# A delta-rule and router kernel whose first stage is put in order by a list scheduler instead of hand-interleaved generators

## The chip, the core and the metric

The kernel runs on one core of a Trainium2 chip. A core has five instruction streams that run side by side and wait for one another through semaphores: TensorE (PE in the profile; PEld is its weight loading), VectorE (DVE), ScalarE (ACT), GpSimd (POOL) and SyncE (SP, which here only issues transfers). SBUF is the on-chip memory of 128 partitions, PSUM the accumulators of TensorE in eight banks. The metric is the device time of the whole program in microseconds (us).

## What is computed

The reference first runs a delta rule over 768 tokens for each of 4 batches and 8 heads of width 48, then sends each token's 384 numbers (8 heads x 48) to its two best of 8 experts.

```python
# delta rule: q, k, v (4, 8, 768, 48), beta (4, 8, 768)
k_n = k / (norm(k) + 1e-6)
for t in range(768):
    y[t] = q[t] @ state
    state = state + beta[t] * outer(k_n[t], v[t] - k_n[t] @ state)
# router: x is y as (3072, 384)
noisy = x @ w_gate + log1p(exp(x @ w_noise)) * noise
top2 and their softmax weights of each token
out[token] += weight * (relu(x @ w1[e]) @ w2[e])      # for its two experts e
```

## The kernel before, in words

The program has two stages. **Stage 1** is the delta rule together with the router's choice; **stage 2** is the eight experts, whose source the change does not touch.

Stage 1 cuts the tokens into 12 chunks of 64. A *unit* is one chunk of one pair of batches (two units a chunk, 24 in all), and a *step* is four units, that is two chunks (six steps, s = 0 to 5). All that depends on k and q alone can be done ahead; only the state must go from chunk to chunk. The pieces are:

- `turned(k)` and `products`: TensorE transposes k (tile `p_t`), ScalarE copies it out (`kT`), TensorE multiplies it with itself (`p_k`), ScalarE copies a part to `at` and the 32-wide diagonal blocks to `gd`.
- `invert(s)`: once a step, VectorE inverts 1024 triangular 32x32 blocks, one column after the other. It transposes `gd` into `t`, finds the lengths of the k (through ScalarE) and the factors `d`, has GpSimd make `low_d`, multiplies `t` by it, and then runs 30 columns of two instructions (`part<-t`, `t<-t,part`). The result is scaled (`scaled`) and transposed twice, into `tt` and `tb`.
- `join(n)`: for each unit, ScalarE copies `tt` into the 64x64 inverse (`w64`, called `w` in the rows), TensorE multiplies `at` by `tb` (`p_x`, first round), ScalarE takes it out negated (`x`), TensorE multiplies again (`p_x`, second round) and ScalarE puts it into `w`.
- `within(n)`: q is transposed (`qT`), multiplied with k (`p_q`), masked by VectorE (`qk`).
- `scale` and `recur`: GpSimd scales `v`; TensorE computes what the state already knows (`p_b`), VectorE subtracts it from `v`, TensorE solves with `w` (`p_u`), ScalarE copies out `u`, TensorE forms the state's increment (`p_s`), VectorE adds it to the state `st`, and GpSimd spreads `st` into the block-diagonal `wide`. This is the chain from chunk to chunk.
- `answer(n)`: TensorE forms the result (`p_y`, from `wide` and from `u`), ScalarE copies `y`, TensorE transposes it (`p_xt`) and multiplies by the gate weights (`p_l`, in the same tile), ScalarE copies the logits.
- `route(s)`: some 25 small VectorE instructions pick the two experts, TensorE counts earlier tokens of each expert (`p_at`), and GpSimd writes the rows into `rows_x` with eight indirect DMAs (`spread`).

Stage 2 reads `rows_x` back (`xr`), so it starts only after the last `spread` has landed.

In what order an engine gets these pieces is set in two places. The source writes them by generators: the loop over chunks calls `take(inverse, 9)`, `take(answers, 3)` and the like between the parts of `recur`, and so mixes inverse, answers, joins and routes by hand. The framework then reorders each engine's instructions by its own estimates. PSUM is shared by two pools: two tiles of one bank (`psum1`) and three of two banks (`psum2`), each given out in the order of the source. At the start ScalarE's queue issues the 16 loads of `beta_b`, and SP issues everything else: k, q and v, the zero-filling of `rows_x` (eight DMAs), the first expert's weights and the zero-filling of the output.

## Time and profile before

| | us |
|---|---|
| runs | 1102.34, 1102.88, 1099.51 |
| median | 1102.34 |
| the profiled execution, its own time | 1099.18 |
| its span | 1097.5 |
| stage 1, until the last count `p_at` starts | 491.9 |
| from there to the end of the span | 605.6 |
| TensorE busy in the span | 889.9 (81%) |
| VectorE busy | 320.2 (29%) |
| ScalarE busy | 253.9 (23%) |
| GpSimd busy | 238.5 (22%) |

The shares are averages over two unlike stages: TensorE is busy nearly all of stage 2, and in stage 1 the work is spread over four engines that hand it on. So the stages are to be read apart. The clock that a row calls PEclk is the one granted to TensorE, as a share of its full speed.

### The profile page before, as it was taken

To read this page: it belongs to the slowest core of one execution; us is meant where nothing else is said; L and a number is where in the kernel's file an instruction comes from. 1 tells how busy PE (TensorE), PEld (TensorE's weight loads), DVE (VectorE), ACT (ScalarE), POOL (GpSimd) and SP (SyncE) were. 2 spreads that over 40 slices of the span, in tenths; PEclk is the share of its full clock that TensorE was granted. 3 is DMA by queue.
4 is the path that set the end of the run, shared out by engine and by line. 5 is a ranking of instruction groups with operands and counts; after the bars stand their busy time and mean duration, and the time that the engine had idled before them with its cause. 6 is when DMAs were issued, how large, how long until landed. Compare 5 with 4: busy or idle time off the path is not lost. (4 is left out here: it accounts for less than half of the span.)

```text
span 1097.5 us, 20220 instructions
## 1 busy us (share of the span) xinstructions
PE 889.9 (81%) x8670; PEld 609.6 (56%) x8670; DVE 320.2 (29%) x916; ACT 253.9 (23%) x621; POOL 238.5 (22%) x297
## 2 busy tenths in 40 slices
PE   3348147786977869672999999999999999999994
PEld 2347046675866758662555555555555555555552
DVE  1777753274573761312002011020120201202000
ACT  3354234442535415110201102002011020110200
POOL 4201111413214231306013012121130121302211
PEclk9657558675576855755999999999999999999997
DMA  5896202312212110106424114241141312301100
GB/s 105 245 365 194 43 2 46 101 36 72 44 31 84 37 63 13 60 1 215 139 86 158 60 45 147 79 143 48 73 155 72 120 56 86 117 8 39 44 23 26
DMA packets 119763, 95.54 MB, mean 87 GB/s; under 512 B 84558, under 2 KB 109676, under 8 KB 119664
## 3 DMA queue, kind: packets, MB, share of 16 engines
q1 hardware_dynamic: 108784, 65.63, 20.5%
q0 software_dynamic: 9984, 28.42, 7.6%
q8 instruction: 70, 1.15, 0.4%
q14 instruction: 29, 0.24, 0.1%
q10 hardware_dynamic: 896, 0.10, 0.1%
HBM read 60.10 MB, written 35.60 MB: 87 GB/s over the span
## 5 line engine op out<-in xcount | busy, mean ns | idle before, releaser
L747 PE MATMUL p_h<-xe,w1e 128*128 128x416 f32 x768 | 270.3, 513 | 6.3 <-DVE xe L741 6.3
L772 PE MATMUL p_o<-w2e,hT 128*128 128x384 f32 x768 | 249.0, 486 | 0.0
L747 PEld LDWEIGHTS p_h<-xe,w1e 128*128 128x128 f32 x768 | 145.3, 190 | 127.0 <-issue 119.7
L772 PEld LDWEIGHTS p_o<-w2e,hT 128*128 128x128 f32 x768 | 145.9, 190 | 102.2 <-issue 2.5
L751 ACT ACTIVATE hT<-p_h 128x416 f32<-128x416 f32 x128 | 66.2, 517 | 491.5 <-PE p_h L747 475.9
L776 DVE SCALAR_TENSOR_TENSOR sums<-p_o,gate,sums 128x384 f32<-128x384 f32 x48 | 29.7, 618 | 449.8 <-PE p_o L772 449.8
L807 POOL DMA_INDIRECT out_dram<-sums,index x56 | 55.1, 984 | 405.0 <-DVE sums L776 382.5
L180 POOL DMA_INDIRECT rows_x<-y,slot x48 | 49.7, 1035 | 91.7 <-issue 42.0
L798 POOL DMA_INDIRECT sums<-out_dram,index x56 | 55.9, 999 | 56.0 <-issue 40.0
L352 DVE TENSOR_TENSOR t<-t,part 128x30 f32<-128x30 f32 (+9 forms) x180 | 61.2, 340 | 4.8
L348 DVE TENSOR_TENSOR part<-t 128x30 f32<-128x30 f32 (+9 forms) x180 | 60.9, 339 | 4.8
L285 PE MATMUL p_q<-qT,kT 64*64 64x64 f32 x768 | 19.0, 258 | 51.1 <-ACT qT L277 49.7
L377 ACT COPY w<-tt 32x256 f32<-32x256 f32 x96 | 38.6, 402 | 55.7 <-DVE tt L363 54.4
L430 PE MATMUL p_y<-u,qk 64*64 64x48 f32 x768 | 45.9, 296 | 1.7 <-issue 1.7
L489 PE MATMUL p_u<-v,w 64*64 64x48 f32 x768 | 39.7, 269 | 9.0 <-ACT y L437 7.1
L285 PEld LDWEIGHTS p_q<-qT,kT 64*64 64x64 f32 x768 | 16.5, 166 | 54.6 <-ACT qT L277 53.0
L430 PEld LDWEIGHTS p_y<-u,qk 64*64 64x64 f32 x768 | 41.9, 212 | 7.1 <-issue 7.1
L463 POOL TENSOR_TENSOR v<-v,norms 128x384 f32<-128x384 f32 x24 | 21.1, 891 | 105.4 <-DMA v<-in_v_dram 90.1
L489 PEld LDWEIGHTS p_u<-v,w 64*64 64x64 f32 x768 | 37.2, 186 | 11.7 <-ACT y L437 6.6
L519 POOL COPY wide<-st 64x384 f32<-64x384 f32 x44 | 23.0, 522 | 91.4 <-DVE st L516 75.6
L383 PE MATMUL p_x<-tb,at 32*32 32x32 f32 x768 | 22.9, 226 | 23.3 <-DVE tb L364 21.5
L737 PE MATMUL p_xt<-ident,xr 128*128 128x128 f32 (+1 forms) x168 | 21.8, 285 | 19.4 <-DMA xr<-rows_x 19.4
(134 smaller groups left out, 862.4 us busy)
## 6 DMA issues: line engine op xcount, KB each, us to landing
w1e<-in_moe_w_dram SPq DMA_DIRECT2D x8, 1536.0 KB
w2e<-in_moe_w_dram SPq DMA_DIRECT2D x8, 1536.0 KB
rows_x<-empty SPq DMA_DIRECT2D x8, 1358.0 KB
xr<-rows_x SPq DMA_DIRECT2D x8, 1164.0 KB
kp<-in_k_dram SPq DMA_DIRECT2D x48, 96.0 KB
qp<-in_q_dram SPq DMA_DIRECT2D x48, 96.0 KB
v<-in_v_dram SPq DMA_DIRECT2D x48, 96.0 KB
out_dram<-empty SPq DMA_DIRECT2D x1, 4608.0 KB
```

The source lines that it names most:

```text
L180: d = nc.gpsimd.indirect_dma_start(out=rows_x, out_offset=bass.IndirectOffsetOnAxis(ap=slot, axis=0), in_=rows, in_offset=None,).ins
L285: nc.tensor.matmul(out[rows_of[b], z, j], lhsT[rows_of[z], j, rows_of[b]], rhs(rows_of[z], j, b), start=(j == 0), stop=(j == NP - 1), skip ...
L348: nc.vector.tensor_tensor(out=part, in0=t[:, j + 1 :, j, None].to_broadcast(shape), in1=t[:, None, j, 0:j].to_broadcast(shape), op=ALU.mult,)
L352: nc.vector.tensor_tensor(out=t[:, j + 1 :, 0:j], in0=t[:, j + 1 :, 0:j], in1=part, op=ALU.add)
L377: nc.scalar.copy(w64[rows, :, cols], tt[rows])
L430: nc.tensor.matmul(p_y[b, h], qk[b, h % 2, h // 2], u[b, h], start=(c == 0 and h == 0), stop=(h == H - 1), skip_group_check=True,)
L489: nc.tensor.matmul(p_u[b, h], w64[b, h], r[b, h], start=(h == 0), stop=(h == H - 1), skip_group_check=True,)
L747: nc.tensor.matmul(p_h, w1e[:, do, fo * 128 : (fo + 1) * 128], xe[:, do, cols], start=(do == 0), stop=(do == KT - 1),)
L751: nc.scalar.activation(hT[:, fo, cols], p_h, ACTF.Relu)
L772: nc.tensor.matmul(p_o, hT[:, fo, i * 128 : (i + 1) * 128], w2e[:, fo], start=(fo == 0), stop=(fo == FT - 1),)
L798: nc.gpsimd.indirect_dma_start(out=got, out_offset=None, in_=out, in_offset=bass.IndirectOffsetOnAxis(ap=index, axis=0), bounds_check=N - ...
L807: nc.gpsimd.indirect_dma_start(out=out, out_offset=bass.IndirectOffsetOnAxis(ap=index, axis=0), in_=got, in_offset=None, bounds_check=N - ...
```

## The change

The change writes stage 1 as some 1340 *jobs*. A job names an engine, a cost in us, what it reads and writes, the PSUM bank it opens, uses or closes, and sometimes a due time; its `emit` holds the instructions. `Jobs.order` is a list scheduler: it keeps a clock for each engine, takes again and again the job that could start first (among those within 0.05 us, the one due earliest), and gives it a free PSUM bank out of four pairs (tiles `pair_112` to `pair_115` in the rows below). The jobs are then emitted in the order of their planned starts, and `tc.manual_schedule` keeps that order on TensorE, ScalarE, VectorE and SP. GpSimd is not in that list, so there the framework goes on choosing.

Besides that:

- the 16 loads of `beta_b` go from ScalarE's queue to SP's, and half of step 0's k loads (four DMAs) go to ScalarE's;
- the zeroing of the borders of `qp` and `w64` goes from GpSimd to VectorE;
- in step 0 half of the `gd` copies and the `low_d` multiply are VectorE's;
- `tb` is transposed ahead of `tt`;
- logits and slots have two buffers each.

```diff
-        psum1 = ictx.enter_context(
-            tc.tile_pool(name="psum1", bufs=2, space=bass.MemoryType.PSUM)
+        psum = ictx.enter_context(
+            tc.tile_pool(name="psum_d", bufs=1, space=bass.MemoryType.PSUM)
         )
-        psum2 = ictx.enter_context(
-            tc.tile_pool(name="psum2", bufs=3, space=bass.MemoryType.PSUM)
-        )
+        jobs = Jobs([psum.tile([128, 2, 512], FP32, name=f"pair{i}") for i in range(4)])
...
-            nc.scalar.dma_start(out=beta_b[i * H : (i + 1) * H], in_=by_block[b, n, c, u])
+                jobs.add(
+                    SP, 0.7,
+                    lambda i=i, at=(b, n, c, u): nc.sync.dma_start(
+                        out=beta_b[i * H : (i + 1) * H], in_=by_block[at]
+                    ),
+                    writes=[("beta", i)], lands=2.5,
+                )
...
+                engine = ACT if name == "k" and n < US and i else SP
+                queue = nc.scalar if engine == ACT else nc.sync
...
+                on, copy = (DVE, nc.vector.tensor_copy) if s == 0 and x % 2 else (
+                    ACT, nc.scalar.copy
+                )
...
+            on = (DVE, 1.25, v_) if s == 0 else (POOL, 2.4, nc.gpsimd)
...
-            nc.vector.transpose(out=tt.rearrange("p h i -> p i h"), in_=scaled)
-            nc.vector.transpose(
-                out=tb.rearrange("p h j -> p j h"), in_=scaled.rearrange("p i j -> p j i")
+            jobs.add(
+                DVE, 1.95,
+                lambda: v_.transpose(out=tbs.rearrange("p h j -> p j h"),
+                                     in_=scaled.rearrange("p i j -> p j i")),
+                reads=["low_d"], writes=["tb"],
+            )
+            jobs.add(
+                DVE, 1.95,
+                lambda: v_.transpose(out=tts.rearrange("p h i -> p i h"), in_=scaled),
+                reads=["low_d"], writes=["tt"],
...
+                        POOL, 1.3, lambda i=i, to=to: spread(ys(s)[:, i], to[:, i : i + 1]),
+                        reads=[("slot", s % 2), meta, ("num", s % 2), ("y", s % 2, i), "clear"],
...
-                if i == 0:
-                    take(answers, 3)
-                    if grams:
-                        products(grams[0])
-                    take(inverse, 9)
-                    take(joins, 2)
-                    take(routes, 3)
...
+            for n in units:
+                join(n)
+            for n in units:
+                recur(n)
+                answer(n)
+            route(s)
+        with tc.manual_schedule(
+            engines={
+                mybir.EngineType.PE, mybir.EngineType.Activation, mybir.EngineType.DVE,
+                mybir.EngineType.SP,
+            }
+        ):
+            jobs.run()
```

The scheduler's inner loop, cut to its core:

```python
for engine in self.ENGINES:
    at = []
    for i in could[engine]:
        start = max(free[engine], ready[i])
        if jobs[i].opens:
            start = max(start, room[0])          # when a PSUM bank comes free
        at.append((start, jobs[i].due, i))
    if at:
        soon = min(at)[0] + self.PATIENCE
        pick = min((x for x in at if x[0] <= soon), key=lambda x: x[1:])
        best = min(best or (1e9,), pick)
```

Three places show how the order moves. In each row stand the line, the operation, and the tile written and the tiles read. First ScalarE's queue at the program's start, before:

```order
L941 UNCONDITIONAL_BRANCH
L247 DMA beta_b<-in_beta_dram 8x6x32 x16
L640 ACT_TABLE_LOAD
L277 COPY kT<-p_t 128x512 x2
L305 COPY at<-p_k 128x256
```

And ScalarE's queue at the start now:

```order
L1227 UNCONDITIONAL_BRANCH
L954 ACT_TABLE_LOAD
L416 DMA kp_116<-in_k_dram 64x8x48
L416 DMA kp_117<-in_k_dram 64x8x48
L416 DMA kp_118<-in_k_dram 64x8x48
L416 DMA kp_119<-in_k_dram 64x8x48
L438 COPY kT_182<-pair_112 128x512
L438 COPY kT_183<-pair_112 128x512
```

Four transfers stand where sixteen stood, and the load of the activation table comes first.

Second, TensorE from a step's first `p_x` (line 383 before, 594 now) on, in step 3. Before, up to the first results `p_y`:

```order
L383 MATMUL p_x<-tb,at 32x32 x32
L285 MATMUL p_b<-st_3378,kT 64x48 x7
L392 MATMUL p_x<-w_0_147,x 32x32 x16
L392 MATMUL p_x<-w_1_150,x 32x32 x16
L285 MATMUL p_b<-st_3378,kT 64x48 x2
L383 MATMUL p_x<-tb,at 32x32 x16
L285 MATMUL p_b<-st_3378,kT 64x48 x5
L383 MATMUL p_x<-tb,at 32x32 x16
L285 MATMUL p_b<-st_3378,kT 64x48 x2
L285 MATMUL p_b<-st_3399,kT 64x48 x2
L392 MATMUL p_x<-w_2_153,x 32x32 x16
L285 MATMUL p_b<-st_3399,kT 64x48 x14
```

Now, from the same place to the first `p_s` (line 707; `p_b` is line 449 with `st`, `p_u` is line 689):

```order
L594 MATMUL pair_112<-tb,at_194 32x32 x16
L594 MATMUL pair_114<-tb,at_195 32x32 x16
L449 MATMUL pair_113<-st_0_220,kT_185 64x48 x16
L594 MATMUL pair_114<-tb,at_196 32x32 x16
L606 MATMUL pair_112<-w_0_148,x_215 32x32 x16
L606 MATMUL pair_114<-w_1_149,x_216 32x32 x16
L594 MATMUL pair_112<-tb,at_197 32x32 x16
L689 MATMUL pair_115<-v_178,w_0_148 64x48 x16
L689 MATMUL pair_115<-v_179,w_1_149 64x48 x16
L707 MATMUL pair_113<-u_212,kp_116 64x48 x16
```

The groups of 16 stay whole, and `p_u` follows the joins of its own two units, where before the answers of the chunk ahead (`p_y`, `p_xt`) came between.

Third, GpSimd between an inverse's `low_d` (line 336 before, 531 now) and its neighbours; `L180` and `L319` are the indirect DMAs of `spread`. Before, around the `low_d` of the fifth inverse and up to its end, where GpSimd sets the diagonal of `t`:

```order
L519 COPY wide_0_171<-st_3399 64x8x48 x2
L336 TENSOR_TENSOR low_d<-low,d 128x1024
L463 TENSOR_TENSOR v<-v,norms 128x384
L519 COPY wide_1_168<-st_3960 64x8x48 x2
L463 TENSOR_TENSOR v<-v,norms 128x384
L519 COPY wide_1_174<-st_3981 64x8x48 x2
L180 DMA rows_x<-y,slot_4093 24576x388
L180 DMA rows_x<-y,slot_4099 24576x388
L356 MEMSET t 128x32
```

Now, from the end of the third inverse to the start of the fourth:

```order
L558 MEMSET t 128x32
L732 COPY wide_0_166<-st_1_218 64x8x48 x2
L660 TENSOR_TENSOR v_180<-v_180,norms_236 128x384
L660 TENSOR_TENSOR v_181<-v_181,norms_236 128x384
L732 COPY wide_0_172<-st_1_221 64x8x48 x2
L319 DMA rows_x<-y_224,slot_0_262 24576x388
...
L319 DMA rows_x<-y_224,slot_1_263 24576x388
L531 TENSOR_TENSOR low_d<-low,d 128x1024
L732 COPY wide_1_167<-st_2_219 64x8x48 x2
```

Before, the `spread` of a step came behind a `low_d`; now all eight stand ahead of one here. Ahead of the third inverse's `low_d` four of eight stand, ahead of the fifth's six, ahead of the sixth's three. On VectorE the multiply that needs `low_d` has the rest of its inverse and the second chunk of the step behind it:

```order
L525 STREAM_TRANSPOSE norms_237<-norm 128x32
L719 TENSOR_TENSOR st_2_219<-pair_115,st_1_218 128x384
L538 TENSOR_TENSOR t<-t,low_d 128x1024
L719 TENSOR_TENSOR st_2_222<-pair_112,st_1_221 128x384
L679 TENSOR_TENSOR v_180<-v_180,pair_115 128x2x4x48
```

The multiply is the third row; the state of the second pair of batches (`st_2_222`) and the next chunk's `v` wait behind it.

## Rows read from the trace of the kernel before

**Rows 1.** The span in 40 equal slices, busy share in tenths, from the page
```profile
PE   3348147786977869672999999999999999999994
DVE  1777753274573761312002011020120201202000
PEclk9657558675576855755999999999999999999997
```

**Rows 2.** Busy time by stretch: engine busy us (instructions), granted clock, DMA share, GB/s
```profile
core 0: us, PE busy (x) PEld busy (x) DVE busy (x) ACT busy (x) POOL busy (x), PEclk, DMA share, GB/s
187.00:252.80 65.80, 52.02 (x1166) 45.91 (x1166) 33.48 (x111) 24.60 (x66) 17.95 (x22) 0.68 0.26 62
252.80:324.90 72.10, 57.78 (x1166) 51.63 (x1166) 39.93 (x123) 30.90 (x82) 19.06 (x23) 0.59 0.21 52
451.30:492.00 40.70, 28.73 (x303) 25.09 (x303) 5.59 (x35) 6.36 (x18) 7.76 (x8) 0.54 0.11 40
520.00:1097.50 577.50, 555.69 (x1809) 314.34 (x1807) 65.51 (x155) 66.18 (x128) 107.45 (x109) 0.99 0.25 83
```

**Rows 3.** The same view, two stretches in which TensorE hardly waits
```profile
286.00:304.00 18.00, 17.67 (x381) 15.73 (x377) 12.15 (x37) 6.92 (x19) 2.35 (x1) 0.50 0.05 11
306.00:318.00 12.00, 9.73 (x313) 8.46 (x312) 6.39 (x21) 8.17 (x22) 2.64 (x4) 0.98 0.26 51
```

**Rows 4.** Timeline, start: start us, us, engine, line, operation, tiles, [idle before <-releaser]
```profile
0.81 12.32 ACTq L247 DMA_DIRECT2D beta_b<-in_beta_dram  x16
13.17 1.28 ACT L640 ACT_TABLE_LOAD   x1 [13.17 <-DMA beta_b<-in_beta_dram]
25.21 1.91 DVE L315 STREAM_TRANSPOSE t<-gd 128x1024 f32<-128x1024 f32 x1 [22.28 <-ACT gd L308]
33.54 1.83 DVE L342 TENSOR_TENSOR t<-t,low_d 128x1024 f32<-128x1024 f32 x1 [3.08 <-POOL low_d L336]
38.90 21.70 SPq L174 DMA_DIRECT2D rows_x<-empty  x8
62.00 1.91 DVE L364 STREAM_TRANSPOSE tb<-scaled 128x1024 f32<-128x1024 f32 x1
109.61 1.89 DVE L364 STREAM_TRANSPOSE tb<-scaled 128x1024 f32<-128x1024 f32 x1
403.77 1.97 DVE L364 STREAM_TRANSPOSE tb<-scaled 128x1024 f32<-128x1024 f32 x1
```

**Rows 5.** Timeline, ScalarE and TensorE around 150 us, where TensorE waits longest
```profile
149.97 0.82 ACT L377 COPY w<-tt 32x256 f32<-32x256 f32 x2 [32.46 <-DVE tt L363]
151.45 1.13 PE L285 MATMUL p_q<-qT,kT 64*64 64x64 f32 x32 [30.71 <-ACT qT L277]
```

**Rows 6.** Groups by line in 0 to 500 us: busy us, mean ns | idle before
```profile
L352 DVE TENSOR_TENSOR t<-t,part 128x30 f32<-128x30 f32 (+9 forms) x180 | 61.2, 340 | 4.8
L377 ACT COPY w<-tt 32x256 f32<-32x256 f32 x96 | 38.6, 402 | 55.7 <-DVE tt L363 54.4
L409 DVE TENSOR_TENSOR qk<-p_q,mask 128x512 f32<-128x512 f32 x24 | 16.4, 682 | 6.3 <-PE p_q L285 6.2
L336 POOL TENSOR_TENSOR low_d<-low,d 128x1024 f32<-128x1024 f32 x6 | 14.1, 2346 | 28.0 <-DVE d L334 28.0
L516 DVE TENSOR_TENSOR st<-p_s,st 128x384 f32<-128x384 f32 x20 | 10.9, 543 | 77.5 <-PE p_s L507 77.5
```

**Rows 7.** Timeline, the end of stage 1 and the start of stage 2
```profile
476.83 0.90 PE L442 MATMUL p_xt<-ident,y 128*128 128x128 f32 x3 [0.58 <-ACT y L437]
483.26 0.90 PE L442 MATMUL p_xt<-ident,y 128*128 128x128 f32 x3 [0.58 <-ACT y L437]
491.90 0.60 PE L593 MATMUL p_at<-r_taken,mask_u 128*128 128x32 f32 x2 [5.65 <-DVE y L535]
495.84 0.96 POOL L180 DMA_INDIRECT rows_x<-y,slot  x1 [30.68 <-issue]
497.11 0.96 POOL L180 DMA_INDIRECT rows_x<-y,slot  x1 [0.30 <-issue]
```

More of the change, by code (lines that the diff above doesn't have):

```diff
@@ new lines, in ring, with per_head, two_banks @@
+        def ring(shape, name, n, zero=None, engine=nc.gpsimd):
+            made = [sb(shape, f"{name}{i}") for i in range(n)]
+            for t in made:
+                for part in zero(t) if zero else ():
+                    engine.memset(part, 0.0)
+            return lambda i: made[i % n]
+        def per_head(p):
+            return p.tile[:, 0 : H * D].rearrange("p (h d) -> p h d", d=D)
+        def two_banks(p, cols):
+            return p.tile[:, :, 0 : NP * cols].rearrange("p z (j d) -> p z j d", d=cols)
@@ new lines, in second, with joined @@
+            def second():
+                for h in range(H):
+                    for up, dn in pairs:
+                        nc.tensor.matmul(
+                            p_x()[up, 1, h], x[dn, h], w64[dn, h, Q:C],
+                            start=(h == 0), stop=(h == H - 1), skip_group_check=True,
+                        )
+            def joined():
+                for up, dn in pairs:
+                    nc.scalar.copy(w64[up, :, Q:C], p_x()[up, 1])
+            w, below = ("w", n % NW), [("w", n % NW, lo) for lo in (Q, C + Q)]
@@ new lines, in multiply @@
+            def multiply():
+                p_l = p_xt.tile[:, KT * 128 : KT * 128 + 2 * E]
+                for do in range(KT):
+                    nc.tensor.matmul(
+                        p_l, xTs(n)[:, do], router["wgn"][:, do],
+                        start=(do == 0), stop=(do == KT - 1),
+                    )
+            reads = [("qT", n % NQ), ("qk", n % NQ), ("u", n % N_U)]
+            if c:
+                reads.append(("wide", z, c % 2))
+            jobs.add(PE, 2.2 if c else 1.3, of_chunk, reads=reads, opens=p_y)
@@ new lines, in answer @@
+            jobs.add(
+                ACT, 0.5,
+                lambda: nc.scalar.copy(y_n, per_head(p_y).rearrange("p h d -> p (h d)")),
+                writes=[y_key], closes=p_y,
+            )
+            jobs.add(PE, 0.6, turn, reads=[y_key], opens=p_xt)
+            jobs.add(
+                ACT, 0.5,
+                lambda: nc.scalar.copy(
+                    xTs(n), p_xt.tile[:, 0 : KT * 128].rearrange("p (t i) -> p t i", i=128)
+                ),
+                writes=[xT_key], uses=p_xt,
+            )
@@ new lines, in answer @@
+            jobs.add(PE, 1.0, multiply, reads=[xT_key, "wgn"], uses=p_xt)
+            jobs.add(
+                ACT, 0.2,
+                lambda: nc.scalar.copy(
+                    logits(s)[:, i],
+                    p_xt.tile[:, KT * 128 : KT * 128 + 2 * E].rearrange(
+                        "p (x e) -> p x e", e=E
+                    ),
+                ),
+                writes=[("logits", s % 2, i)], closes=p_xt,
+            )
+        small = {x: sb([128, Q], x) for x in ("ss", "root", "norm", "d")}
@@ new lines, in rows, with weights @@
+            def rows():
+                p_at = p.tile[:, 0 : US * E].rearrange("p (u e) -> p u e", e=E)
+                vv(at, p_at, part[:, None, :].to_broadcast([128, US, E]), ALU.add)
+                for hit, to in zip((hit0, hit1), slot):
+                    vv(mine, hit, at, ALU.mult)
+                    nc.vector.tensor_reduce(out=row, in_=mine, axis=AX.X, op=ALU.add)
+                    nc.vector.tensor_copy(to, row)
+            def weights():
+                nc.vector.tensor_scalar(
+                    out=den, in0=p1, scalar1=1.0, scalar2=1e-9, op0=ALU.add, op1=ALU.add
+                )
+                nc.vector.reciprocal(den, den)
+                vv(gate1, p1, den, ALU.mult)
+                vv(gate0, den, gate1, ALU.subtract)
@@ new lines, in counted @@
+            def counted():
+                nc.vector.tensor_reduce(
+                    out=r_count, in_=taken.rearrange("p u e -> p e u"), axis=AX.X, op=ALU.add
+                )
+                vv(before, before, r_count, ALU.add)
+            every_logit = [("logits", s % 2, i) for i in range(US)]
+            meta = ("meta", s % 2)
+            jobs.add(
+                POOL, 0.2,
+                lambda: nc.gpsimd.tensor_copy(
+                    num, number.rearrange("p c u -> p (c u)")[:, every]
+                ),
+                writes=[("num", s % 2)],
+            )
```

871 lines of the change are left out of this document (490 added, 381 removed).

## The prediction

> **What bounds the kernel now.** I read the 40 slices first, since the shares of the whole span mix two stages. TensorE is at 9 tenths or more from the 19th slice on and at a clock of 9 tenths, and between 3 and 8 before that, at 4 to 7 tenths [rows 1]. So the second stage is bound by TensorE (555.69 of 577.50 us busy at a clock of 0.99 [rows 2]), the change leaves its source alone, and I carry its time over. The first stage ends when the last count `p_at` starts, at 491.90, and the last `spread` and the read-back of `rows_x` follow from there [rows 7]. Whatever is gained must bring that moment forward.
>
> Inside stage 1 the landmark is the end of `tb`, which is the end of an inverse: 63.9 for the first, 111.5 for the second and 405.7 for the sixth [rows 4]. Four steps lie between the last two, 73.6 us each. No engine needs that long. TensorE is busy 52.02 of 65.80 us and 57.78 of 72.10, VectorE 33.48 and 39.93, ScalarE and GpSimd less [rows 2]. The rest is handing on in a poor order. The plainest case: ScalarE stood 32.46 us before a `w` copy whose `tt` was not there, with the copy of `qT` queued behind it, and TensorE waited 30.71 us for that `qT` [rows 5]. A better order can win only up to what the slowest engine needs alone, so I work out that bound for each engine, and then the path in the order that the change fixes.
>
> **TensorE's price depends on its clock.** The two middle stretches of [rows 2] hold the same 1166 matmuls: 52.02 us at 0.68 and 57.78 at 0.59. A line in one over the clock through both (14.2 + 25.7/clock) gives 39.9 us a step wholly at 2.4 GHz and 65.6 at 1.2. What the clock will be is the largest unknown. In 286 to 304 TensorE was busy 17.67 of 18 us and had 0.50, that is the lower level throughout; in 306 to 318, busy 9.73 of 12, it had 0.98 [rows 3]. So a full queue did not bring the high level there, and I take about 0.62, the middle of the two steps: 55.6 us.
>
> The Trainium skill ("TensorE: Matmul & The Clock Gate", "Loop structure matters more than you think") says that whether matmuls stay at the fast clock is a matter of keeping them back to back. By that rule the denser order would lift the clock; the first row of [rows 3] disagrees, and the rule's result is the first rival.
>
> **The start.** ScalarE issues 16 `beta_b` loads in 12.32 us, loads its table at 13.17 and only then copies; `t<-gd` starts at 25.21 after 22.28 us of idle VectorE [rows 4]. Now ScalarE issues four loads (3.1 us at 0.77 each) and the table (1.28), so it is free at about 5.5. When k lands the rows do not show, only that it was there by 14.46, when the first copy followed right behind the table; with half of its loads on each queue I take 6 to 10. The copies took it some 11 us (14.46, right behind the table, to 25.21); with half of the `gd` copies on VectorE 7 to 9. That puts `t<-gd` between 13 and 19 (23 if k really needs till 14.46); I take 16, a gain of 9. The betas on SP (16 more issues, about 12 us) are needed only in the lengths, behind `t<-gd`. The zeroing that VectorE takes over lies in its idle 22 us; were that cover gone it would cost about 2.
>
> From `t<-gd` to the end of `tb` the first inverse took 38.7 us. The wait of 3.08 for GpSimd's `low_d` [rows 4] goes, a multiply on VectorE of about 1.5 comes, and `tt` (1.9) moves behind `tb`: 35.2, so `tb` ends at 51. The second inverse took 47.6 us after the first; I keep that and add 2 for the loads of `v`. SP now has those 16 betas and step 1's q ahead of the 21.70 us of `rows_x` clears [rows 4], and step 1's `v` behind the clears and the weights; that could cost 0 to 10, once. The second `tb` ends at 101.
>
> **A step in the new order.** VectorE works in the fixed order, so I add it up from one `tb` to the next. Behind the multiply `t<-t,low_d` lie: multiply, the 30 columns (60 instructions of 0.34 us [rows 6] and the gaps between them) and `scaled`, together 25.9 (from 33.54 to 62.00 is 28.5, less one `qk` of 0.68 and `tt` of 1.9); `tb` 1.9; one `st`, two `v` (0.54 each; the subtraction is of the same shape) and four `qk` (0.68 each), 4.3; and the router's small operations, 4.8 of the 5.59 that the last stretch shows [rows 2, 4, 6]. That is 36.9 us.
>
> Ahead of that multiply stand `tt`, `t<-gd`, one `st`, two `v` and the gates: 6.6 us. Only then can GpSimd start the `spread`s, because the gates are part of the rows, and GpSimd's order, which the change leaves to the framework, puts 4, 8, 6 and 3 of them ahead of the next `low_d`. One `spread` takes 1.27 us from start to start [rows 7], `low_d` 2.35 [rows 6]. So the multiply starts at 9.0 + 1.27n after `tb`, and a step takes at least 51.0, 56.1, 53.5 and 49.7 us. Without any `spread` ahead it would be some 46: this is a **new wait** that the change makes, and behind it on VectorE stand the second `st` and the second chunk's `v`, hence TensorE's second `p_u`.
>
> TensorE needs 55.6 at the middle clock, and cannot have zero idle time: at each `tb` it waits for the first `x` and `w` copies, and ScalarE's 16 `w` copies of 0.40 a step [rows 6] stand between join and `p_u`. I put 2 to 3 us on that. **TensorE is later than VectorE's sum in each step**, so the steps are 58, 59 (where eight `spread`s also hold VectorE), 58, and 54 for the last, in which no k of a further step is multiplied. That is 229 in place of 294, and the sixth `tb` ends at 330 in place of 405.7.
>
> **The end of stage 1.** From there before needed 86.2 us to `p_at`, since work of the chunk before was still queued ahead. Now the last step's joins, two chunks of `p_b`, `p_u` and one `p_s` (18 to 24 us by clock, estimated from TensorE's steps), four answers, and the router are left. An answer took 6.43 us from `p_xt` to `p_xt`, with 0.58 waiting for `y` [rows 7]; with two of them in flight I count 5 each. The router waited 5.65 before `p_at` [rows 7]. 21 + 20 + 1.5 + 6 is about 49, so `p_at` starts at 379.
>
> **The sum.** 491.9 less 379 is 113. The profiled execution took 1099.18 us (span 1097.5), so the same execution would take 986. The median of the three runs, 1102.34, lies 3.2 above the profiled one; I say 988.
>
> **The rivals.**
>
> *The clock rises.* If fewer gaps keep TensorE at 2.4 GHz, its 39.9 us a step vanish behind VectorE, whose four steps give 210 by the floors above, 216 with 1.5 us of waiting each. The end shrinks to 40, since the matmuls of the last answers are halved. `p_at` then starts at 101 + 216 + 40 = 357: **967**. For it: 0.98 in 306 to 318. Against it: 0.50 in the densest stretch, and 0.54 in the last [rows 2, 3]. Two in ten.
>
> *TensorE stays at 1.2 GHz.* 65.6 a step and 1 of handing on, 62 in the last, 55 at the end: 101 + 262 + 55 = 418, a gain of 74: **1028**. For it: the same 0.50 row. The order groups `p_x`, `p_u` and `p_y`, which is what ran there. Two in ten.
>
> *Slower than before.* The place is GpSimd's queue between two inverses. The order is fixed on four engines and cannot give way there: `low_d` waits for all `spread`s ahead of it, these for the router's gates, the router for the last answer's logits, and VectorE's multiply holds the second chunk. If that ring closes, TensorE stands still while VectorE waits and the other way about. It decides once the four steps reach 491.9 - 49 - 101 = 342, 85.5 each: TensorE at 65.6 and idle 20 us in every step, as long as GpSimd takes for eight `spread`s, `low_d` and what is ahead (19). At 88 a step the result is **1110**. Against it: only one of four steps has all eight ahead, and TensorE has products of the next steps queued meanwhile. Five in a hundred.
>
> *The late loads of `v`.* All of the 10 us instead of 2 gives 996; this is inside the forecast. That the order isn't what the change says is excluded for the four fixed engines by the order of the built program; what is not fixed, GpSimd's, is priced above.
>
> **How the numbers follow.** Forecast 0.53, high clock 0.2, low clock 0.2, slower 0.05, and 0.02 for a result within 0.3% of before (3.3 us, about what a measurement of this kernel can tell from no change), the point at which the ring almost closes. Range: the high clock's 967 less 15, for a start 5 us earlier and one `spread` fewer ahead in each step; the low clock's 1028 plus 8 for the late `v`: 952 to 1036. Faster 0.93, within 0.02, slower 0.05.
>
> **What would show it.** Right: `t<-gd` at 13 to 19 and the first `tb` at about 51; steps of 54 to 60 between `tb`s; TensorE busy over 90% of a step at a clock near 0.6; VectorE's longest idle in front of `t<-t,low_d`, released by GpSimd, longest in the fourth inverse; stage 2 unchanged at about 606 us from `p_at`. Wrong: a clock of 0.9 in stage 1 with VectorE full (first rival), steps of 66 at 0.5 (second), VectorE and TensorE idle by turns over 15 us a step (third), or `t<-gd` still after 20.

## The result, and the profile after

| | before | changed |
|---|---|---|
| runs, us | 1102.34, 1102.88, 1099.51, 1097.93 | 1009.23, 1008.37, 1008.77, 1004.28 |
| median | 1100.92 | 1008.57 |
| the profiled execution (its span) | 1099.18 (1097.5) | 1009.23 (1007.5) |
| `p_at` of the last step starts | 491.9 | 404.1 |
| from there to the end of the span | 605.6 | 603.4 |

The changed kernel takes 0.9155 of the time [0.912, 0.919]: 92 us less, where 114 (to 988) had been forecast. Of the 90 us between the two spans 87.8 are the earlier end of stage 1.

The busy shares of the 40 slices of the changed kernel, in tenths (a slice is now 25.2 us):

```profile
PE   4368778676968767199999999999999999999995
DVE  6957768496785832210200200201201102002001
PEclk7757667596875858599999999999999999999998
```

Against [rows 1], VectorE stands at 4 to 9 in the first 14 slices (stage 1 ends in the 17th), and TensorE at much the same tenths as before, for fewer slices. The stretches between the ends of `tb`, and stage 2, in the columns of [rows 2]:

```profile
core 0: us, PE busy (x) PEld busy (x) DVE busy (x) ACT busy (x) POOL busy (x), PEclk, DMA share, GB/s
0.00:50.70 50.70, 21.22 (x432) 17.15 (x432) 39.39 (x123) 19.64 (x47) 13.18 (x39) 0.73 0.56 102
50.70:109.90 59.20, 45.10 (x938) 41.62 (x938) 39.09 (x111) 29.14 (x79) 5.62 (x7) 0.63 0.99 333
109.90:173.20 63.30, 50.62 (x1194) 46.14 (x1193) 44.87 (x123) 30.34 (x81) 24.04 (x29) 0.68 0.33 76
173.20:235.00 61.80, 45.89 (x1170) 41.45 (x1169) 43.91 (x123) 30.93 (x82) 19.59 (x23) 0.75 0.28 67
235.00:295.00 60.00, 45.86 (x1167) 41.07 (x1166) 43.56 (x123) 30.89 (x82) 19.24 (x23) 0.75 0.23 57
295.00:355.50 60.50, 46.18 (x1066) 40.62 (x1064) 45.35 (x122) 23.89 (x62) 19.84 (x23) 0.70 0.22 55
355.50:404.10 48.60, 34.34 (x868) 31.21 (x868) 12.62 (x39) 18.90 (x52) 10.77 (x14) 0.68 0.10 35
430.00:1007.50 577.50, 558.70 (x1817) 316.07 (x1815) 67.00 (x158) 66.18 (x128) 108.97 (x110) 0.99 0.26 84
```

A step went from 73.6 us to some 61. No engine fills one: TensorE is busy 45.9 of 61.8 at a clock of 0.75, VectorE 43.9. What VectorE waits for is seen in its timeline around the second of the four steps' multiplies by `low_d`, with the first `t<-gd`, the last multiply and the last `p_at` (idle time before and its releaser in brackets):

```profile
16.73 1.91 DVE L495 STREAM_TRANSPOSE t<-gd 128x1024 f32<-128x1024 f32 x1
...
194.46 0.56 DVE L719 TENSOR_TENSOR st<-pair,st 128x384 f32<-128x384 f32 x1 [10.06 <-PE pair L707]
194.93 1.22 DVE L538 TENSOR_TENSOR t<-t,low_d 128x1024 f32<-128x1024 f32 x1
...
307.55 1.18 DVE L538 TENSOR_TENSOR t<-t,low_d 128x1024 f32<-128x1024 f32 x1
...
404.13 0.64 PE L882 MATMUL pair<-r_taken,mask_u 128*128 128x32 f32 x2 [5.62 <-DVE r_taken L833]
```

`t<-gd` answers to 25.21 in [rows 4], `p_at` to 491.90 in [rows 7]. The multiply at 194.93 comes 21.7 us after its `tb`, but it has no wait of its own: VectorE stood 10.06 us before the state `st` ahead of it, for the products of TensorE. So the longest wait was where the prediction put it, and the engine that came last was another.

What TensorE did in those 10 us stands in its timeline, here with GpSimd's (the lines 689 and 707 are `p_u` and `p_s`):

```profile
181.66 1.75 PE L689 MATMUL pair<-v,w 64*64 64x48 f32 x26
183.69 0.43 PE L689 MATMUL pair<-v,w 64*64 64x48 f32 x3 [0.28 <-issue]
...
185.86 0.36 PE L689 MATMUL pair<-v,w 64*64 64x48 f32 x3 [0.96 <-issue]
187.29 0.46 PE L689 MATMUL pair<-v,w 64*64 64x48 f32 x4 [1.06 <-issue]
...
191.60 1.09 PE L689 MATMUL pair<-v,w 64*64 64x48 f32 x15 [0.47 <-issue]
193.26 1.10 PE L707 MATMUL pair<-u,kp 64*64 64x48 f32 x32 [0.57 <-ACT u L696]
...
180.15 1.03 POOL L319 DMA_INDIRECT rows_x<-y,slot  x1 [3.60 <-DVE before L833]
...
189.15 0.97 POOL L319 DMA_INDIRECT rows_x<-y,slot  x1 [0.30 <-issue]
190.19 2.34 POOL L531 TENSOR_TENSOR low_d<-low,d 128x1024 f32<-128x1024 f32 x1
```

The 64 matmuls of one `p_u` came in pieces of 3 to 5 with about 1 us between them, for which the trace shows no releaser, and took 11 us, while GpSimd issued eight `spread`s (180.15 to 190.1). The same happens, with pauses of 0.3 to 0.5 us, to `p_s` in the last of the four steps. But the last row counts too: behind the `spread`s `low_d` was ready only at 192.53, 19.3 us after `tb`, so without the pieces this multiply could have started 2.4 us earlier and no more. Two suspects therefore stand side by side: the `spread`s delay `low_d` by their place in GpSimd's queue, which the prediction says, and they go together with a slower TensorE, which it doesn't.

### The profile page after: what moved, and what is told of

Same layout as the page of the kernel before. It is cut to its first block, busy times and chain, and to the rows that moved or that the text cites. A ratio compares the mean times of both kernels' runs of the same rounds, so it can differ in the third digit from the quotient of the medians.

```text
span 1007.5 us, 20278 instructions
## 1 busy us (share of the span) xinstructions
PE 854.3 (85%) x8670; PEld 581.5 (58%) x8670; DVE 341.5 (34%) x941; ACT 250.0 (25%) x613; POOL 235.8 (23%) x280
## 5 line engine op out<-in xcount | busy, mean ns | idle before, releaser
L1084 POOL DMA_INDIRECT sums<-out_dram,index x56 | 56.0, 999 | 55.5 <-issue 39.7
L546 DVE TENSOR_TENSOR part<-t 128x30 f32<-128x30 f32 (+9 forms) x180 | 63.9, 355 | 5.3
L319 POOL DMA_INDIRECT rows_x<-y,slot x48 | 47.9, 999 | 56.6 <-DVE r_count L910 29.5
L689 PE MATMUL pair<-v,w 64*64 64x48 f32 x768 | 43.0, 270 | 13.8 <-issue 13.2
L689 PEld LDWEIGHTS pair<-v,w 64*64 64x64 f32 x768 | 39.1, 184 | 16.8 <-issue 16.2
L732 POOL COPY wide<-st 64x384 f32<-64x384 f32 x44 | 29.0, 659 | 63.1 <-DVE st L719 57.4
L449 PE MATMUL pair<-qT,kT 64*64 64x64 f32 x768 | 21.3, 269 | 17.9 <-DVE qk L641 9.0
L478 ACT COPY gd<-pair 32x256 f32<-32x256 f32 x88 | 31.9, 362 | 17.2 <-PE pair L449 14.2
L1023 PEld LDWEIGHTS p_xt<-ident,xr 128*128 128x128 f32 (+1 forms) x168 | 19.5, 151 | 23.4 <-issue 23.4
L606 PE MATMUL pair<-w,x 32*32 32x32 f32 x768 | 25.2, 229 | 8.8 <-ACT x L601 3.3
L449 PE MATMUL pair<-kT 64*64 64x64 f32 x768 | 20.4, 273 | 13.4 <-ACT kT L438 7.6
```

The costliest lines, as they stand in the source:

```text
L319: d = nc.gpsimd.indirect_dma_start(out=rows_x, out_offset=bass.IndirectOffsetOnAxis(ap=slot, axis=0), in_=rows, in_offset=None,).ins
L449: nc.tensor.matmul(out[rows_of[b], z, j], lhsT[rows_of[z], j, rows_of[b]], rhs(rows_of[z], j, b), start=(j == 0), stop=(j == NP - 1), skip ...
L546: v_.tensor_tensor(out=part, in0=t_inv[:, j + 1 :, j, None].to_broadcast(shape), in1=t_inv[:, None, j, 0:j].to_broadcast(shape), op=ALU.mult,)
L689: nc.tensor.matmul(per_head(p_u)[b, h], w64[b, h], v_n[b, h], start=(h == 0), stop=(h == H - 1), skip_group_check=True,)
L1023: nc.tensor.transpose(p_xt[:, do, 0:rows], xr[0:rows, i, do * 128 : (do + 1) * 128], ident[0:rows, 0:rows],)
L1084: nc.gpsimd.indirect_dma_start(out=got, out_offset=None, in_=out, in_offset=bass.IndirectOffsetOnAxis(ap=index, axis=0), bounds_check=N - ...
```

## The experiments

There were three sets of runs, each on one chip and with its own runs of the kernel before. In the first set before's median was 1105.75, in the second 1076.05, in the third 1075.58, so times are compared within a set, and ratios across sets. The changed kernel itself ran again only in the third; in the first, stretches are set beside those of the first result, whose before (1100.92) is near.

### First set: are the spreads the cost, and what do the other parts give alone?

**Without the spreads of steps 0 to 4** (on the changed kernel):

```diff
-            for i in range(US):
+            for i in range(US if s + 1 == NS else 0):
                 for to in slot:
                     jobs.add(
                         POOL, 1.3, lambda i=i, to=to: spread(ys(s)[:, i], to[:, i : i + 1]),
```

> The changed kernel without the spreads of steps 0 to 4 (the rows of those tokens are not written to rows_x; the last step's are). Theory A (the spreads cost twice: low_d queues behind them, and TensorE's matmuls stutter while they run): the four steps from the second to the sixth tb fall from 61.4 to about 53 us each, the 64 matmuls of p_u that took 11 us in the second of them take under 3, the end from the sixth tb to p_at falls from 48.7 to about 42; time about 966. Theory B (the steps are long because VectorE's fixed order waits for the state and TensorE's own work is what it is): steps stay within 2 us, time above 1000.

Measured 978.50, ratio 0.885 [0.880, 0.890]. The steps are 57.5, 53.2, 54.2 and 51.1, together 216 in place of 245.6, and the end 43.4 in place of 48.7; `p_u` runs through in one piece of 3.65 us. `p_at` starts at 366.7 in place of 404.1, so the `spread`s cost stage 1 some 37 us on this chip; from there to the end it is 6 us more than before (609.4 against 603.4), which no run explains, and so the time misses the expected 966. This doesn't yet say whether by their place in the queue or by the pieces, since both went.

**`low_d` on VectorE in every step**, which takes it out of GpSimd's queue:

```diff
-            on = (DVE, 1.25, v_) if s == 0 else (POOL, 2.4, nc.gpsimd)
+            on = (DVE, 1.25, v_)
```

> The changed kernel with the low_d multiply on VectorE in every step (in the change only in step 0), so that no VectorE instruction waits for GpSimd's queue; the spreads stay. If the queue ahead of low_d is what costs: steps of about 54, time about 980. If TensorE's stutter during the spreads is what costs (theory A's larger part): steps of 59 to 62, time 1000 to 1010, with p_u still in pieces.

Measured 1006.39, ratio 0.910 [0.905, 0.916]. The steps fell to 59.2, 58.2, 60.4 and 58.1, but the end rose to 57.1: TensorE's work is still in pieces beside most runs of `spread`s, and the pieces moved with them. So on this chip the queue ahead of `low_d` alone doesn't explain the 37 us. How much of them it explains this run can't say: the scheduler planned anew, and VectorE's order is another one.

**The head alone** (on the kernel before): the betas on SP behind k, half of the first k loads on ScalarE.

```diff
-        for i in range(128 // H):
-            b, n, c, u = i // 8, i // 4 % 2, i // 2 % 2, i % 2
-            nc.scalar.dma_start(out=beta_b[i * H : (i + 1) * H], in_=by_block[b, n, c, u])
...
-                nc.sync.dma_start(
+                queue = nc.scalar if name == "k" and n < US and i else nc.sync
+                queue.dma_start(
...
             load(n, "k")
+        for i in range(128 // H):
+            b, n, c, u = i // 8, i // 4 % 2, i // 2 % 2, i % 2
+            nc.sync.dma_start(out=beta_b[i * H : (i + 1) * H], in_=by_block[b, n, c, u])
```

> The kernel before with one part of the change alone: the 16 beta loads on SP behind the k loads, and half of step 0's k loads on ScalarE behind its table load. Theory: t<-gd moves from 25.2 to about 17 and the 8 us carry through to the end, since the inverses follow one another: about 1092. Rival: they are lost at the first place where the stage waits for something else (the loads behind the clears, TensorE idle between 108 and 151 us): 1098 to 1102.

Measured 1106.10, ratio 1.001 [0.999, 1.004]: nothing. The first `tb` ends at 54.2 in place of 63.9, the second at 107.2 (111.5), the third at 162.4 (161.7). The timeline of ScalarE and TensorE shows where it went, as in [rows 5] but longer:

```profile
145.66 2.88 ACT L375 COPY w<-tt 32x256 f32<-32x256 f32 x7 [33.06 <-DVE tt L361]
149.21 1.13 PE L283 MATMUL p_q<-qT,kT 64*64 64x64 f32 x32 [45.18 <-ACT qT L275]
```

The framework, choosing anew, put both copies of `qT` behind the `w` copies; TensorE waited 45 us for them in place of 31.

**The spreads two at a time**, as jobs behind columns 5, 12, 18 and 24 of the next inverse, so that the scheduler plans everything anew:

```diff
+                if s > 1 and j in AT:
+                    for go in later[s - 2][2 * AT.index(j) : 2 * AT.index(j) + 2]:
+                        go(("column", s, j))
...
```

> The changed kernel with the spreads of step s held back and paced: two at a time behind columns 5, 12, 18 and 24 of inverse s+2 (step 4's behind the u copies of step 5). Theory A: low_d no longer queues, and TensorE does not stutter since only two spreads follow one another: steps of 53 to 54, end of 45; time about 975. If TensorE stutters at every spread, the stall only moves: steps of 58 to 61, time 995 to 1008.

Measured 1005.69, ratio 0.909 [0.904, 0.914]; it can't be read as meant. The steps are 54, 76.8, 42.6 and 71.1, because the new plan moved other things too: the copies of `gd` and the router's chain stand ahead of the joins. One row of VectorE shows it:

```profile
172.19 0.19 DVE L842 TENSOR_TENSOR r_at<-pair,part 128x32 f32<-128x32 f32 x1 [9.24 <-PE pair L598]
```

The lesson was to hold the order of the other engines and move the `spread`s alone. One thing can still be read, since this chip is one with pieces: TensorE's pauses behind a pair, and behind two pairs that follow at once (four `spread`s, 376.08 to 380.9).

```profile
126.89 1.26 PE L610 MATMUL pair<-w,x 32*32 32x32 f32 x38 [0.56 <-issue]
...
381.82 0.35 PE L770 MATMUL pair<-u,qk 64*64 64x48 f32 x2 [1.10 <-issue]
```

Beside its 16 pairs the pauses (those above 0.15 us) sum to 4.3 us, none above 0.6; beside each of the two runs of four to 2.3 and 2.5 us, up to 1.1. So pairs break TensorE's work too, but less in this run.

### Second set: the same order, and no order

**Paced, in the same order.** The jobs and their plan are those of the changed kernel; only where a `spread` is written changes (with the small copy of its row numbers), and it waits for the mark that it stands behind. TensorE, ScalarE and VectorE keep their order, instruction by instruction.

```diff
+                if j in (5, 12, 18, 24):
+                    flush(s - 2, mark)
...
+        def flush(s, mark):
+            for _ in range(2):
+                if held_back and held_back[0][0] <= s:
+                    x, i, to = held_back.pop(0)
+                    out_row(x, i, to)
+                    if mark is not None:
+                        tc.add_manual_dep(written[-1], mark.name, SYNC, reason="paced")
...
-                        POOL, 1.3, lambda i=i, to=to: spread(ys(s)[:, i], to[:, i : i + 1]),
+                        POOL, 1.3, lambda i=i, to=to: put(s, i, to),
```

> The changed kernel with the order of TensorE, ScalarE, VectorE and SP as it is, and only the spreads of steps 0 to 4 held back: two at a time behind columns 5, 12, 18 and 24 of inverse s+2, step 4's two at a time behind a w copy, two u copies and a y copy of the last step. So low_d stands ahead of them in GpSimd's queue. If the spreads' queue and TensorE's stutter are the cause and the earlier paced run only lost by its new order on the other engines: steps of 53 to 55 as in the run without spreads, end 44 to 46, time 972 to 982. If pairs of spreads stutter TensorE as much as eight in a row: 995 to 1010.

Measured 977.16, ratio 0.907 [0.900, 0.914]. The steps are 59.4, 53.9, 53.9 and 53.9, the end 44.1: near the steps of the kernel without `spread`s in the first set, with every row written. Whether pairs cost TensorE less than runs of eight this run doesn't tell: on this chip even the kernel with free order (below), whose `spread`s come in runs of up to eight, shows only three pauses beside them, 2.1 us in all. One of these steps (columns as above):

```profile
168.10:222.00 53.90, 42.56 (x1162) 39.20 (x1161) 44.01 (x123) 30.70 (x82) 20.91 (x26) 0.78 0.31 75
```

**Paced, with eight buffers for `v`** in place of four:

```diff
-        NQ, N_U, N_ST = 2 * NU, 2 * NU + 1, 3
+        NQ, NV, N_U, N_ST = 2 * NU, 4 * NU, 2 * NU + 1, 3
...
-        vs = ring([128, H, D], "v", NQ)
+        vs = ring([128, H, D], "v", NV)
```

> The kernel e9 with eight buffers for v in place of four, so that step 1's v is loaded ahead of the clears of rows_x and does not wait behind them; this lets the list scheduler choose anew. If the late v is what makes the first of the four steps 3 to 4 us longer than the others without spreads: 968 to 978, 4 under e9. If not: as e9 within 3.

Measured 972.12, ratio 0.902 [0.894, 0.909]: 5.0 us below the last. The first of the four steps went from 59.4 to 56.8. VectorE and ScalarE keep their order, so the 5 us come with the earlier loads of `v` (and with GpSimd's order, which isn't fixed); where they fall isn't settled, since the same kernel has 58.3 in that step when it runs again below.

**The jobs, without the fixed order** (the changed kernel, the framework choosing on all engines):

```diff
-        with tc.manual_schedule(
-            engines={
-                mybir.EngineType.PE, mybir.EngineType.Activation, mybir.EngineType.DVE,
-                mybir.EngineType.SP,
-            }
-        ):
-            jobs.run()
+        jobs.run()
```

> The changed kernel without the fixed order: the jobs are emitted in the scheduler's order with its PSUM banks, and the framework reorders all engines as it did before. If the order of emission and the banks carry the gain: 995 to 1025. If it is the fixing of the order on four engines: 1060 to 1100.

Measured 1013.32, ratio 0.940 [0.931, 0.949], against 0.918 for the changed kernel in the third set: fixing the order is worth about 24 us of the gain (7 to 40 by the outer ends of the two intervals), and all else in the change some 63. Only the start is measured apart (the last run below); how the rest divides among the order of writing, the four PSUM pairs, `tb` ahead of `tt` and the second buffers, no run shows. Without it ScalarE's old wait is back:

```profile
157.65 3.78 ACT L620 COPY w<-tt 32x256 f32<-32x256 f32 x9 [29.19 <-DVE tt L576]
```

**Before's order of writing, fixed** (the kernel before, under the same fixing on four engines):

```diff
-    with ExitStack() as ictx:
+    with ExitStack() as ictx, tc.manual_schedule(
+        engines={
+            mybir.EngineType.PE, mybir.EngineType.Activation, mybir.EngineType.DVE,
+            mybir.EngineType.SP,
+        }
+    ):
         weights = deltanet(ictx)
```

> The kernel before with its order fixed on TensorE, ScalarE, VectorE and SP just as the generators write it. If the framework's reordering was what kept the stage slow (a qT queued behind w copies that wait): 1050 to 1080. If the interleaving by hand is itself the loss: 1095 to 1130.

Measured 1115.64, ratio 1.035 [1.025, 1.045]. The interleaving by hand, as it stands, is the poorer order; the framework's reordering had won about 40 us from it. To fix an order helps only where the order is good.

### Third set: the changed kernel, the best version, and two parts

**The changed kernel again**, unchanged, so that the third set has its own measure.

> The changed kernel once more, beside the paced ones on one chip. Its sixth tb ends at 355 and p_at at 404 us of its span as in its first profile; the ratio to before comes out within 1% of the 0.9155 of the first comparison if chips do not matter, and higher than that if this chip is one on which before runs in 1076.

Measured 988.87, ratio 0.918 [0.912, 0.924]. The ratio is that of the first result, the time is 20 us lower, as before's is 25, and `p_at` starts at 386.9 and not at the expected 404. The same `p_u` as above, the four steps' multiplies, all released by GpSimd, and, in the first of these steps, two subtractions of VectorE and what GpSimd does ahead of them:

```profile
181.72 3.65 PE L689 MATMUL pair<-v,w 64*64 64x48 f32 x64
...
128.08 1.50 DVE L538 TENSOR_TENSOR t<-t,low_d 128x1024 f32<-128x1024 f32 x1 [1.18 <-POOL low_d L531]
192.36 1.49 DVE L538 TENSOR_TENSOR t<-t,low_d 128x1024 f32<-128x1024 f32 x1 [4.61 <-POOL low_d L531]
248.25 1.23 DVE L538 TENSOR_TENSOR t<-t,low_d 128x1024 f32<-128x1024 f32 x1 [0.21 <-POOL low_d L531]
299.83 1.23 DVE L538 TENSOR_TENSOR t<-t,low_d 128x1024 f32<-128x1024 f32 x1 [2.82 <-POOL low_d L531]
...
133.71 0.56 DVE L679 TENSOR_TENSOR v<-v,pair 128x384 f32<-128x384 f32 x1 [2.69 <-POOL v L660]
138.29 0.56 DVE L679 TENSOR_TENSOR v<-v,pair 128x384 f32<-128x384 f32 x1 [3.59 <-POOL v L660]
...
131.78 1.01 POOL L319 DMA_INDIRECT rows_x<-y,slot  x1 [0.28 <-POOL wide L732]
132.85 0.82 POOL L660 TENSOR_TENSOR v<-v,norms 128x384 f32<-128x384 f32 x1
...
137.42 0.84 POOL L660 TENSOR_TENSOR v<-v,norms 128x384 f32<-128x384 f32 x1
```

On this chip `p_u` runs through while the same eight `spread`s are issued beside it, and now each multiply is released by `low_d`, as predicted. So the pieces depend on the chip or its condition, and the queue belongs to the kernel. It holds back more than `low_d`: in the first step the scaled `v` of two units stands between and behind the step's other four `spread`s, and VectorE waits 6.3 us for it, against 1.2 for `low_d` there.

**Eight spreads in a row behind column 5**: behind `low_d` as in the paced kernel, but not spread out.

```diff
-                if j in (5, 12, 18, 24):
-                    flush(s - 2, mark)
+                if j == 5:
+                    for _ in range(4):
+                        flush(s - 2, mark)
```

> The paced kernel (four v buffers) with all eight spreads of a step behind column 5 of the inverse instead of two behind each of four columns: low_d stays ahead of them, so only TensorE's stutter differs from the paced one. If eight in a row make TensorE stutter and that reaches the path: steps of 56 to 58 in place of 53.9, time 985 to 1000. If it was the queue ahead of low_d alone: steps of 54, time 975 to 980.

Measured 975.95, ratio 0.907 [0.902, 0.913], 12.9 us below the changed kernel on the same chip. The steps are 56.5, 54.6, 55.5 and 52.8 in place of 64.2, 58.5, 55.8 and 55.2, so more than half of the gain lies in the first, where both the wait for `low_d` and the two for `v` are gone. Where there are no pieces, it is the place behind `low_d` and `v` that counts and not the pacing (whose ratio in the second set was 0.907 as well).

**The best version**: the paced kernel with eight `v` buffers once more, beside the changed kernel.

> The paced kernel with eight buffers for v, on the same chip as the changed kernel: 30 to 40 us less than it (966 to 978 where the changed kernel has 1004 to 1009) if the spreads and the late v are the cause; under 10 less if the gain of the last comparison came from another chip.

Measured 971.34, ratio 0.904 [0.898, 0.910]: 17.5 us (1.8%) below the changed kernel on the same chip, and the fastest. The expected 30 to 40 didn't come, since the changed kernel itself takes 989 where there are no pieces. VectorE in the second of the four steps, ahead of which `tb` ends at 164.5:

```profile
174.04 0.35 DVE L508 RECIPROCAL norm<-root 128x32 f32<-128x32 f32 x1 [3.10 <-ACT root L503]
178.79 0.56 DVE L725 TENSOR_TENSOR st<-pair,st 128x384 f32<-128x384 f32 x1 [2.77 <-PE pair L713]
179.26 1.78 DVE L538 TENSOR_TENSOR t<-t,low_d 128x1024 f32<-128x1024 f32 x1
```

The multiply starts 14.8 us after `tb`, in place of 19.3. GpSimd is out of the way; what is late next is ScalarE's `root`, and then TensorE's `p_s`.

**The head undone** (the changed kernel with its betas on ScalarE ahead of k, and all of k on SP):

```diff
-                jobs.add(
-                    SP, 0.7,
-                    lambda i=i, at=(b, n, c, u): nc.sync.dma_start(
-                        out=beta_b[i * H : (i + 1) * H], in_=by_block[at]
-                    ),
-                    writes=[("beta", i)], lands=2.5,
+                nc.scalar.dma_start(
+                    out=beta_b[i * H : (i + 1) * H], in_=by_block[b, n, c, u]
                 )
...
-                engine = ACT if name == "k" and n < US and i else SP
+                engine = SP
...
+        load_beta()
         nc.scalar.preload_act_table_set("natural_log_exp_and_others")
...
-        load_beta()
```

> The changed kernel with its start undone: the 16 beta loads on ScalarE's queue ahead of the table load, all k loads on SP. t<-gd at 25 in place of 16.7. If the order is tight from the first inverse on, the 8 us reach the end: 1012 to 1018 where the changed kernel has 1004 to 1009. If the wait for step 1's v hides them: within 3 us of the changed kernel.

Measured 999.39, ratio 0.930 [0.924, 0.936], 10.5 us above the changed kernel (5.3 by `p_at` in the two profiles, 392.2 against 386.9). The first `tb` comes 11 us later here. So a gain at the start that gives nothing in the old order gives 5 to 10 us in the new one.

## Why the prediction was right, and where not

The landmarks of the sum, with the execution of the first result and that of the changed kernel in the third set:

| | forecast | first result | third set |
|---|---|---|---|
| `t<-gd` | 16 | 16.7 | 16.3 |
| first `tb` ends | 51 | 50.7 | 50.3 |
| second | 101 | 109.9 | 108.8 |
| the four steps | 58, 59, 58, 54 | 63.3, 61.8, 60.0, 60.5 | 64.2, 58.5, 55.8, 55.2 |
| sixth `tb` ends | 330 | 355.5 | 342.5 |
| from there to `p_at` | 49 | 48.7 | 44.4 |
| the multiply, after `tb` | 14.1, 19.2, 16.6, 12.8 | 19.6, 21.7, 21.4, 12.6 | 19.3, 19.3, 16.7, 12.6 |

In the first result `p_at` came 25 us after the forecast: 9 of them in the second inverse and 16.5 in the four steps. Stage 2 gave 2 back. So the time lies where the forecast allows, but what set the steps was not what the forecast said: how near it came is in part luck.

- **The start** was right to within 1 us. That its gain goes through to the end in full, as the sum has it, holds only in the new order: the loads alone gave nothing in the kernel before, and 5 to 10 of 11 us in the changed one. **The end of stage 1** (49 forecast, 48.7 measured) fits by luck: in the third set, without pieces, it is 44.4.
- **"The second inverse took 47.6 us after the first; I keep that"** is the step that failed first. It took 59.2. The 47.6 belonged to what before ran there, and the order moves other work in. The first count `p_at`, of step 0's router, on the kernel before:

```profile
63.90:111.50 47.60, 36.01 (x878) 31.89 (x878) 33.33 (x84) 27.13 (x71) 6.10 (x9) 0.67 0.81 258
...
186.87 0.45 PE L593 MATMUL p_at<-r_taken,mask_u 128*128 128x32 f32 x2 [1.50 <-DVE r_taken L535]
```

  and on the changed kernel, with what VectorE waits for in that inverse:

```profile
102.84 0.64 PE L882 MATMUL pair<-r_taken,mask_u 128*128 128x32 f32 x2 [3.58 <-DVE part L546]
...
60.29 0.35 DVE L508 RECIPROCAL norm<-root 128x32 f32<-128x32 f32 x1 [3.92 <-ACT root L503]
67.57 0.56 DVE L723 COPY st<-pair 128x384 f32<-128x384 f32 x1 [3.04 <-PE pair L707]
95.63 0.18 DVE L845 TENSOR_SCALAR r_w<-r_u 128x32 f32<-128x32 f32 x1 [4.46 <-ACT r_u L842]
```

  Step 0's recurrence, answers and route all lie inside it now, 84 us earlier than before. VectorE has 5.8 us more of work there (39.1 against 33.3), and stands idle 5.8 us more. Without `spread`s it still took 56.4 and with eight `v` buffers 57.4 (58.2 without, on that chip), so these are 3 us of it at most.
- **"TensorE is later than VectorE's sum in each step"** is the step that failed next. Its price came from a clock of 0.62; the stretches show 0.68 to 0.75, and the prediction's own line gives 48.5 us at 0.75, where 45.9 were measured. In the first result VectorE did wait for TensorE in each step (4.41, 10.06, 7.92 and 7.68 us for `p_s`), and the pieces lengthened these waits: in the third set they are 1.64, 2.71, 2.71 and 1.45. There the steps are VectorE's chain, with the queue ahead of the multiply and waits that the floors leave out; that the sums of 58 or 59 lie near one of its steps, 58.5, is luck. What lies behind the multiply, 36.9 by the prediction, was 39.1 to 42.6 there, and 44.9 in the first step, with the two waits for GpSimd's `v`.
- **The clock.** On the changed kernel TensorE hardly waits in the second and third of these stretches, of which the third holds four answers; the first is that of the pieces:

```profile
181.00:193.00 12.00, 6.41 (x92) 5.34 (x88) 1.83 (x8) 2.30 (x8) 9.33 (x9) 0.50 0.36 132
193.00:200.00 7.00, 6.74 (x228) 6.43 (x232) 3.73 (x7) 6.04 (x16) 4.66 (x7) 0.50 0.62 116
205.00:219.00 14.00, 13.42 (x242) 12.10 (x236) 12.97 (x32) 5.87 (x18) 1.66 (x2) 1.00 0.15 30
```

  The clock stood at its lower level (0.50) through the pieces, in which TensorE was busy 6.41 of 12 us, and through the dense 7 us behind them; in the dense 14 us of the last row it had the upper one. The Trainium skill ("TensorE: Matmul & The Clock Gate", "Loop structure matters more than you think") says that matmuls that stay back to back stay warm. The last row agrees; the dense 18 us of before [rows 3], at 0.50 throughout, don't. The first rival was right about the clock's direction (0.68 to 0.75 in the steps, where 0.62 was taken), and for the third set right that VectorE's chain then sets the steps. Its time, 967, was too low because that chain took 234 us in place of 216, the second inverse 58.5 in place of 50, and the end 44.4 in place of 40.
- **The queue ahead of `low_d`** was right. In the third set the three multiplies with eight, six and three `spread`s ahead start within 0.2 us of the floors 19.2, 16.6 and 12.8. In the step with four, VectorE waits for `low_d` too, but 5 us after the floor of 14.1: the prediction lets the first `spread` start 6.6 us after `tb`, and it started after 11.9 there (120.67), since VectorE came to the gates only at 119.4, having waited 2.57 for a `p_b`. Taking the `spread`s from their places gave back 12.9 us; a part of these is the wait for `v` behind the other four, which the prediction has in no term. It is a cost that the change still has, not one that it removes: GpSimd is the one engine whose order the change left open.
- **The late `v`** was right in kind: 5 us in all, against 2 in the sum and a range of 0 to 10.
- **The pieces** were in no term. Steps two to four of the first result are 12.8 us longer than the third set's (182.3 against 169.5), and the end 4.3; TensorE's pauses without a releaser there sum to 12.1 and 4.7 us, so they can be the whole difference. Why the kernel before was 25 us slower there too they don't explain: its profile has 4 us of them beside its `spread`s.
- **Slower than before**, by a ring through GpSimd's queue, did not come: in the third set TensorE's longest single wait in the four steps was 4.9 us.
- **Smaller slips**, on which nothing hangs: in [rows 1] TensorE is at 9 tenths from the 20th slice on, at 1 to 9 before, and the clock there at 5 to 9. Two `qk`, not one, lie between 33.54 and 62.00 in before, which takes 0.7 us off the 36.9. Four steps of 88 us give 1112 and not 1110, and the two reasons named for the 15 us below 967 come to 10.

## What to carry to other kernels

When an order is fixed on all engines but one, look at what that one puts ahead of its short, awaited instructions: here runs of indirect DMAs, 1.27 us from start to start, stood ahead of a 2.35 us product and of 0.8 us ones on which the longest chain waited, and moving them behind these was worth 13 us. Time won at the start of such a pipeline survives only as far as the order behind it is tight (0 us in one order, 5 to 10 in the other), and a stretch's old duration can't be kept in a sum when the order moves other work into it. Measure the kernel before beside each version: the same two kernels took 1101 and 1009 us the first time, and 1076 and 989 in the third set, at the same ratio.

## What the runs showed of the hardware

In the first result TensorE's small matmuls came in pieces of 3 to 5, with pauses of about 1 us that no semaphore of the trace explains, beginning a few `spread`s into a run and ending within 2 us of it; one `p_u` of 64 matmuls took 11 us in place of 3.65. The kernel before has a few too, here beside its fifth run of `spread`s (455.3 to 465.2):

```profile
463.94 0.49 PE L430 MATMUL p_y<-u,qk 64*64 64x48 f32 x4 [0.72 <-issue]
465.39 0.24 PE L430 MATMUL p_y<-u,qk 64*64 64x48 f32 x1 [0.96 <-issue]
```

On the chip of the third set the same instructions beside the same `spread`s ran through, and on that of the second there was little of it (2.1 us in the kernel with free order). In the first set, where before took 1105.75 us (1100.92 in the first result), there were no pieces without the `spread`s, with `low_d` on VectorE they stayed, and in the run that wrote the rows two at a time they were shorter beside pairs than beside runs of four: they go with the indirect DMAs and not with GpSimd's product. Not every pause without a releaser is of this kind: between 66 and 81 us the changed kernel has three in both its profiles (2.33, 2.85 and 1.89 us in the first), where no `spread` is under way and the DMA engines move some 355 GB/s. What inside the chip links pauses and transfers, and whether it is the chip or a condition of it, stays open; the version paced in the same order wasn't run where the pieces are.
